# Four small moves in the order of transfers and splits of a fused attention and MLP kernel

## The chip, the cores and the metric

The kernel runs on one core of a Trainium2 chip. The metric is the time of one execution in microseconds of device time, the median of several. All data are float32; matmuls take operands that are split into a high and a low part (fp32r), so that one product is three matmuls.

## The reference, cut to what matters

```
xn  = layernorm(x)                                  # x: 1 x 2048 x 512
qkv = xn @ wqkv                                     # 32 heads of 16
p   = softmax(q k^T / 4)                            # per head, 2048 x 2048
s   = (p v) @ wo
h   = relu(xn @ w1 + b1) ** 2                       # 2048 x 1792
g   = silu(h @ w2 + b2)
out = x + s * g
```

## The kernel before

**Work.** Attention is cut into 32 units: a unit is four heads (a quad, `qd`) and 512 queries (`qc`), so u = 4 qd + qc. A unit has two passes over the keys. The max pass (`max_mm`, L308) multiplies a Q tile `qm` with a K tile `ka` and lets VectorE take the maximum over 512 keys (L323). When a unit's 64 maxima are there, `shift` (L352) turns them into a negated shift, which is stored to DRAM (`keep`, L362, the tensor `sh_d`) and fetched back into rows 48 and 49 of the unit's two exp tiles `qe` (`back`, L367, by `shift_rows`, L377, four transfers of 4 KB). The exp pass (`exp_mm`, L1179) multiplies `ka` with `qe`; the added rows subtract the maximum, and ScalarE takes the exp of it (L1199) into a tile `pt`. `pv_step` multiplies the exps with V two slots later (L387).

**Slots.** The main loop (L1528) counts slots `st`; 16 slots are one unit of the exp pass. A unit's max pass runs some 24 slots ahead (`LEAD`), counted as g = st + 24. In the loop, slots 4 to 451 also hold the MLP, in blocks of four slots (`long_slots`) and single slots; slots 454 to 485 hold the first part of the output projection (`wo_part`, L710), two slots to a tile of 128 rows; from slot 486 on there is no max pass left. In the two slots of `PAIR` (484 and 485) the last four max matmuls are done; the string `order` there says in which sequence exp matmuls ("s") and max matmuls ("m") stand beside the projection's own nine.

**The lead.** Before the loop, `lead_rounds` (L1316) runs the rest of the QKV projection in rounds of one matmul in either half of the array, with max matmuls of the first units and some first exps between them. Six rounds are a step; `now` counts steps there and slots in the loop, and `later(n, fn)` (L198) puts a call off by n of them. Every QKV tile ends in `qk_done` (L998): ScalarE copies it out of PSUM (L1004), POOL splits it into a buffer `hl` of three (L95, L96), SP stores it two steps later (`qk_store`, L942). The last but one tile of the lead, the K columns of the last eight heads, goes through `qk_done_last` (L1008) with its own buffers, and is stored at slot 6 (L1539). The first exp of the lead is in step 45.

**Q loads.** `max_end(g)` (L327) stands at the end of each slot. With s the place of g in its group of 16, it asks for the two exp tiles of unit u (six transfers of 32 KB each, `load_q_pair`) at two places s, and for the two max tiles of unit u + 1 at two others. When a unit's maxima are complete it puts the unit on the list `late` with the g at which `shift` is due. For units after the first the exp tiles' places 12 and 14 are the slots 16u - 12 and 16u - 10, and the places 7 and 9 the slots 16u - 17 and 16u - 15. The max pass is seven slots further ahead than g says, since the lead did 62 max matmuls in either half; it starts on a unit's max tiles in the fourth slot after a multiple of 16.

**Queues.** SP issues nearly all transfers, in the order in which they stand in the program; an issue waits until the data it reads are written, its target is free, and now and then for an earlier transfer. What stands behind it waits too. ScalarE issues only two of the last stores.

**The MLP's start and the projection.** `mlp_tasks` (L467) first calls `load_xc(0)` (L497), which asks in four transfers of 256 KB for the first 256 tokens of the layernorm's result, `xc`; the first MLP block, in slot 4, reads it and the w1 tiles that POOL splits (`split_w1`). The projection asks for its input tiles `oc` in `wo_load` (L665): for the second 512 tokens three of 512 KB, at slots 456, 457 and 458, read from slot 462 on. Between them stand the 13 small loads of `wo_small` (slot 457) and `keep` and `back` of a unit.

Of the kernel before, what the change touches and what calls it, by code (L numbers as in the profile page):

```python
# [10 lines left out]
F32R = mybir.dt.float32r  # L11
# [6 lines left out]
P = 128  # L18
# [9 lines left out]
NU = NQ * 4  # L28
# [25 lines left out]
def kernel(  # L54
# [11 lines left out]
    nc = tc.nc  # L66
# [24 lines left out]
    def split(dst, raw, hi_act=False, lo=None):  # L91
        if hi_act:
            nc.scalar.activation(dst[0], raw, AF.Copy)
        else:
            nc.gpsimd.tensor_scalar(dst[0], raw, 1.0, 0.0, op0=ALU.mult, op1=ALU.add)  # L95
        (lo or nc.gpsimd).tensor_tensor(  # L96
            dst[1], raw, dst[0].bitcast(F32), op=ALU.subtract
        )
# [12 lines left out]
    with ExitStack() as ph:  # L111
# [10 lines left out]
        def ring(name):  # L122
            t = rot[name][turn[name] % len(rot[name])]
            turn[name] += 1
            return t
# [17 lines left out]
        qms = {}  # L143
# [3 lines left out]
        def load_head(t, j, src_d, h, parts, cols):  # L147
            for n, i in enumerate(parts):
                nc.sync.dma_start(
                    t[64 * j + DH * n : 64 * j + DH * (n + 1), :].bitcast(F32),  # L150
                    src_d[h // 8][i, (h % 8) * DH : (h % 8 + 1) * DH, cols],
                )

        def load_k(qd, n):

            p, j, i = n // 6, n // 3 % 2, n % 3
            if n % 6 == 0:
                kas[qd, p] = ring("ka")
            h = 4 * qd + 2 * p + j
            nc.sync.dma_start(  # L160
                kas[qd, p][64 * j + DH * i : 64 * j + DH * (i + 1), :].bitcast(F32),
                k_d[h // 8][i % 2, (h % 8) * DH : (h % 8 + 1) * DH, :],
            )
# [20 lines left out]
        def load_q_pair(u, name, p, tiles):  # L184
                qd, qc = divmod(u, 4)
                t = ring(name)
                for j in range(2):
                    load_head(
                        t, j, q_d, 4 * qd + 2 * p + j, (0, 0, 1), slice(qc * 512, (qc + 1) * 512)
                    )  # L190
                tiles.append(t)

        late = []
# [4 lines left out]
        def later(n, fn):  # L198
            if n:
                waiting.append((now[0] + n, fn))  # L200
            else:
                fn()
# [124 lines left out]
        def max_end(g):  # L327
            for u in [u for u, n in left.items() if n == 0]:
                del left[u]
                m4 = m4s[u % 2]  # L330
                nc.vector.tensor_reduce(m4[:, :16], mxs[u], axis=AX.X, op=ALU.max)
                mxs[u] = m4
                late.append((g + (6 if u else 2), u))
            u, s = divmod(g, 16)
            if u >= NU:
                return
            qd, qc = divmod(u, 4)
            if qc == 2 and qd + 1 < NQ and s % 2 == 0:
                load_k(qd + 1, s // 2)
            if qc == 3 and qd + 1 < NQ and s % 2 == 0 and s < 8:  # L340
                load_k(qd + 1, 8 + s // 2)
            at = (12, 14) if u else (7, 8)
            if s in at:
                load_q_pair(u, "qe", at.index(s), qes.setdefault(u, []))
            if s in (6, 10) and u + 1 < NU:
                load_q_pair(u + 1, "qm", s // 10, qms.setdefault(u + 1, []))

        def shift_due(g):
            if late and late[0][0] <= g:
                shift(late.pop(0)[1])  # L350

        def shift(u):  # L352
            tr = sp.tile([P, 32], F32, name="tr", bufs=1)
            nc.vector.transpose(tr, mxs[u])
            sh = sp.tile([P, 2, 32], F32R, name="sh", bufs=1)
            nc.vector.tensor_scalar(sh[:, 0], tr, -1.0, None, op0=ALU.mult)
            nc.vector.scalar_tensor_tensor(
                sh[:, 1], tr, -1.0, sh[:, 0].bitcast(F32),
                op0=ALU.mult, op1=ALU.subtract,
            )  # L360

            def keep():  # L362
                nc.sync.dma_start(
                    sh_d[u].rearrange("b c i n -> (b c) i n"), sh.bitcast(F32)
                )

            def back():  # L367
                for p in range(2):
                    for i in range(2):
                        shift_rows(u, p, i)  # L370

            later(1, keep)
            later(2, back)

        to_block = []

# [90 lines left out]
        def mlp_tasks(mp):  # L467
# [29 lines left out]
            def load_xc(c):  # L497
                    xc = xp.tile([P, 2, KO, CW], F32R, name="xc")
                    for k in (0, 2) if c == 0 else (0,):
                        kos = slice(k, k + 2 if c == 0 else KO)  # L500
                        for i in range(2):
                            nc.sync.dma_start(
                                xc[:, i, kos].bitcast(F32), xn_d[i, :, kos, c * CW : (c + 1) * CW]
                            )
                    state["xc"] = xc
# [402 lines left out]
        pools = {}  # L908
# [30 lines left out]
        def qk_store(m, c, hl):  # L939
            cs = slice(c * 512, (c + 1) * 512)  # L940
            dst = q_d[m] if m < 4 else k_d[m - 4]
            nc.sync.dma_start(dst[:, :, cs].rearrange("i p n -> p i n"), hl.bitcast(F32))  # L942
# [64 lines left out]

        def qk_done_last(m, c, ps):  # L1008

            hl = pools["n"].tile([P, 2, 512], F32R, name="hl")  # L1010
            raw = sp.tile([P, 512], F32, name="ot", bufs=1)
            nc.scalar.activation(raw, ps, AF.Copy)
            split((hl[:, 0], hl[:, 1]), raw)
            last_store.append(lambda: qk_store(m, c, hl))

        def qk_first():
            tiles = [qk_tile(m, 0) for m in (4, 0)]
# [97 lines left out]
        last_store = []  # L1115
# [47 lines left out]
        order = []  # L1163
# [58 lines left out]
        for i in range(NT + 3):  # L1222
# [38 lines left out]
            if i >= 7 and (i - 3) % 4 == 3:  # L1261
                c = (i - 3) // 4
# [3 lines left out]
            if i >= 3 and (i - 3) % 4 == 3:  # L1266
                c = (i - 3) // 4
# [22 lines left out]
        at = order.index(("v", 2, 0)) + 1  # L1290
# [120 lines left out]
        def slot(st, mms, post):  # L1411

            g = st + LEAD
            lane = (st + flip[0]) % 2
            kb0 = st - lane
            for kb in (kb0, kb0 + 1):
                pts.setdefault(kb, {})
            spare = st >= LAST_MAX
            ex = [
                lambda j=j, kb=kb: exp_mm(kb, j, pts[kb], spare and next(odd))  # L1420
                for kb in (kb0, kb0 + 1) for j in (1 - lane, 3 - lane) if j not in pts[kb]
            ]
            if st in TWO:

                for _ in range(2):
                    max_mm(lane)
                    ex.pop(0)()
                if ex:
                    kb, j = (kb0 + 1, 2 + lane) if lane else (kb0, lane)
                    exp_mm(kb, j, pts[kb], True)  # L1430
                    ex.pop(0)()
                last_use[0] = None
                max_end(g)
                return
            k = 0 if spare else max(0, (8 - len(mms)) // 2)
            own = [lambda: max_mm(lane) for _ in range(k)] + mms
            if spare and lane == 0:

                own.append(lambda: exp_mm(kb0, 0, pts[kb0], next(odd)))
            assert k == 0 or st not in PAIR  # L1440
            mx = [] if spare else [lambda: max_mm(1 - lane) for _ in range(2 if st in PAIR else 4 - k)]
            order = "s" * len(ex) if spare else {0: "smsmsmsm", 1: "smsmssm"}[k]
            if not spare and post is None:

                if k == 0:
                    order = "msmsmsms"
                elif lane and k == 1 and to_block:
                    order = "smsmsms"
            if st in PAIR:
                order = "smsmss"  # L1450
            other = [(ex if o == "s" else mx).pop(0) for o in order]
            other[-1:-1] = [None] * (len(own) - len(other))
            use = None
            for i in range(len(other)):
                if i < len(own):
                    own[i]()
                if spare and lane == 0 and i == len(mms) - 1:

                    use = nc.vector.tensor_scalar(seen, done_d[0][:, :1], 1.0, 0.0, op0=ALU.mult, op1=ALU.add)
                if other[i] is not None:  # L1460
                    follow = other[i]()
                    if i >= len(own) - 1 and use is None:
                        use = follow
            last_use[0] = None if post is not None or spare and lane else use
            if post is not None:
                post()
            max_end(g)
# [117 lines left out]
```

## Time and profile before

| what | us |
|---|---|
| median of 3 runs | 1646.31 (1646.17 to 1649.19) |
| the profiled execution, as a run | 1644.67 |
| its span, first to last instruction | 1642.6 |
| TensorE busy in the span | 1619.3 (99%) |
| VectorE busy | 1359.5 (83%) |
| ScalarE busy | 1190.1 (72%) |
| POOL busy | 523.0 (32%) |
| mean granted TensorE clock | 0.997 |

The profile is one execution. A row of its timeline has the start, the duration, the engine, the line, and in brackets the idle time of that engine just before and what ended it. Groups of equal neighbours are one row (x6). SPq and ACTq are DMA requests as these engines issue them: the time there is that of the issue, not of the transfer. PE is TensorE's matmuls and PEld its weight loads. The granted clock is the share of full speed that TensorE was given.

### The profile page before, as it was taken

Reading aid. Unit: us, or ns where it says so; the run is one execution under the profiler, and the core shown is the slowest. Engines: PE = TensorE matmul, PEld = TensorE weight load, DVE = VectorE, ACT = ScalarE, POOL = GpSimd, SP = SyncE. Lnnn points to the kernel's source line nnn. Section 1 sums busy time; section 2 is a strip of 40 time slices with the busy share of each in tenths; the row PEclk is TensorE's granted clock in tenths of the full one; section 3 lists DMA queues with packets and bytes.
Section 4 is the critical chain, followed back from the end, with each engine's and each line's share of the span. In section 5 each row is a group of like instructions: output and inputs, shape, how many; then the busy total and the mean of one; then the engine's idle time right before and its main releaser. Section 6 shows DMA issues by size and latency. Waiting matters only on the chain.

```text
span 1642.6 us, 36131 instructions
## 1 busy us (share of the span) xinstructions
PE 1619.3 (99%) x13684; PEld 940.6 (57%) x13684; DVE 1359.5 (83%) x2346; ACT 1190.1 (72%) x2351; POOL 523.0 (32%) x547
## 2 busy tenths in 40 slices
PE   7999999999999999999999999999999999999998
PEld 6898665556555654664466456645655565454543
DVE  6486788888888888888888888888888889886744
ACT  7212677777777777877777777777777777776786
POOL 6436568122212311331133112311321224125421
PEclk9999999999999999999999999999999999999999
DMA  6787565424332433433343324323532353137554
GB/s 226 217 277 248 186 184 153 132 85 126 77 106 82 128 80 87 127 90 82 100 122 107 87 74 141 102 67 87 147 97 67 85 150 81 54 114 218 168 179 154
DMA packets 163941, 209.22 MB, mean 127 GB/s; under 512 B 59448, under 2 KB 78392, under 8 KB 162232
## 3 DMA queue, kind: packets, MB, share of 16 engines
q1 hardware_dynamic: 163480, 206.40, 43.1%
q8 instruction: 108, 1.77, 0.4%
q14 instruction: 65, 0.53, 0.1%
q10 hardware_dynamic: 288, 0.52, 0.1%
HBM read 149.95 MB, written 56.61 MB: 126 GB/s over the span
## 4 chain that ended last, share of the span: by engine, by line
PE 96%; DMA 2%; DVE 1%; SPq 0%; issue 0%; ACT 0%; DVEq 0%; ACTq 0%
PE po L387 31%; PE pd_t L254 19%; PE pm_t L316 16%; PE se L1187 14%; PE pd_t L222 6%; PE pm_t L1065 3%; PE se L1035 1%; PE pd_t L1065 1%; PE se L987 1%; PE se L316 1%; DVE mx L323 1%; DMA oc<-on_d 1%; PE pm_t L1187 0%; DMA sh_d<-sh 0%; PE pm_t L1149 0%; PE pd_t L1035 0%
## 5 line engine op out<-in xcount | busy, mean ns | idle before, releaser
L323 DVE TENSOR_REDUCE mx<-pm_t 128x1 f32<-128x512 f32 x1927 | 1197.3, 684 | 172.8 <-PE pm_t L316 86.7
L1199 ACT ACTIVATE pt<-se 128x512 f32<-128x512 f32 x1996 | 1043.3, 617 | 261.8 <-PE se L1187 217.2
L316 PE MATMUL pm_t<-ka,qm 64*128 64x512 f32 x1927 | 770.5, 420 | 0.7 <-DVE mx L323 0.5
L1187 PE MATMUL se<-qe,ka 64*128 64x512 f32 x1996 | 672.6, 396 | 0.9 <-DMA qe<-sh_d 0.6
L387 PE MATMUL po<-pt,v 128*32 128x512 f32 x4096 | 546.1, 605 | 0.0
L316 PEld LDWEIGHTS pm_t<-ka,qm 64*128 64x128 f32 x1927 | 338.5, 184 | 239.0 <-DVE mx L323 226.8
L254 PEld LDWEIGHTS pd_t<-xc,w1s 64*128 64x128 f32 x2688 | 334.2, 187 | 96.6 <-issue 89.3
L254 PE MATMUL pd_t<-xc,w1s 64*128 64x256 f32 x2688 | 380.9, 288 | 1.7 <-DMA xc<-xn_d 0.8
L1187 PEld LDWEIGHTS se<-qe,ka 64*128 64x128 f32 x1996 | 337.2, 185 | 19.1 <-ACT pt L1199 1.2
L254 PE MATMUL pd_t<-w2t,hT 64*128 64x512 f32 x1080 | 300.5, 410 | 0.0
L254 PEld LDWEIGHTS pd_t<-w2t,hT 64*128 64x128 f32 x1080 | 179.1, 184 | 82.8 <-issue 75.5
L545 POOL TENSOR_TENSOR r<-r 128x512 f32<-128x512 f32 x56 | 58.2, 1040 | 376.5 <-ACT r L542 376.5
L387 PEld LDWEIGHTS po<-pt,v 128*32 128x32 f32 x4096 | 81.0, 108 | 159.1 <-issue 136.5
L564 POOL TENSOR_TENSOR u<-u,b_t 128x512 f32<-128x512 f32 x16 | 20.6, 1286 | 327.2 <-ACT u L563 293.3
L425 POOL TENSOR_TENSOR ot<-ot,hl 128x512 f32<-128x512 f32 x31 | 39.8, 1284 | 204.4 <-DMA hl<-r_d 160.3
L323 DVE TENSOR_REDUCE mx<-se 128x1 f32<-128x512 f32 x121 | 77.9, 686 | 30.8 <-PE se L316 25.7
L222 PE MATMUL pd_t<-wot,oc 64*128 64x512 f32 x336 | 92.0, 410 | 3.8 <-DMA oc<-on_d 3.5
L222 PEld LDWEIGHTS pd_t<-wot,oc 64*128 64x128 f32 x336 | 58.9, 186 | 51.5 <-ACT pt L1199 12.6
L542 ACT ACTIVATE r<-pd_t,b_t 128x256 f32<-128x256 f32 x112 | 46.9, 470 | 57.1 <-PE pd_t L254 57.1
L1065 PE MATMUL pm_t<-xT,wr_t 64*128 64x512 f32 x408 | 75.0, 391 | 0.0
L96 POOL TENSOR_TENSOR hT<-r,hT 128x512 fp32r<-128x512 f32 x56 | 72.3, 1290 | 4.7
L222 PE MATMUL pd_t<-w2t,hT 64*128 64x512 f32 x264 | 68.8, 393 | 0.0
(131 smaller groups left out, 1066.1 us busy)
## 6 DMA issues: line engine op xcount, KB each, us to landing
w1s<-w_d SPq DMA_DIRECT2D x196, 256.0 KB
qm<-q_d SPq DMA_DIRECT2D x384, 32.0 KB
ka<-k_d SPq DMA_DIRECT2D x96, 128.0 KB
qe<-q_d SPq DMA_DIRECT2D x384, 32.0 KB
k_d<-hl SPq DMA_DIRECT2D x16, 512.0 KB
q_d<-hl SPq DMA_DIRECT2D x16, 512.0 KB
xn_d<-xT SPq DMA_DIRECT2D x8, 1024.0 KB
g<-g_d SPq DMA_DIRECT2D x32, 256.0 KB
```

What stands on the lines that cost most here:

```text
L96: (lo or nc.gpsimd).tensor_tensor(dst[1], raw, dst[0].bitcast(F32), op=ALU.subtract)
L222: mm = nc.tensor.matmul(out_, lh(r), rh(r), start=first_ and lane == 0, stop=last_ and lane == 1, skip_group_check=True,)
L254: mm = nc.tensor.matmul(out_, lh(r), rh(r), start=first_ and lane == 0, stop=last_ and lane == 1, skip_group_check=True,)
L316: nc.tensor.matmul(ps, qms[u][p][64 * j : 64 * j + 64, qb * P : (qb + 1) * P], kas[qd, p][64 * j : 64 * j + 64, kc * 512 : (kc + 1) * 512] ...
L323: return nc.vector.tensor_reduce(mxs[u][:, c, kc : kc + 1], ps, axis=AX.X, op=ALU.max)
L387: nc.tensor.matmul(po[32 * j : 32 * j + 32, :], vs[qd][:, (4 * kb + j) * VW : (4 * kb + j) * VW + 32], pts[j], start=(kb == 0), stop=(kb = ...
L425: nc.gpsimd.tensor_tensor(ot, ot, hl[:, 1].bitcast(F32), op=ALU.mult)
L542: nc.scalar.activation(r[:, i], ps[:, i * CW : (i + 1) * CW], AF.Relu, bias=b1_t[:, fo : fo + 1])
L545: nc.gpsimd.tensor_tensor(r, r, r, op=ALU.mult)
L1065: mm = nc.tensor.matmul(out_, lh(r), rh(r), start=first_ and lane == first, stop=last_ and lane != first, skip_group_check=True,)
L1187: nc.tensor.matmul(se, kas[qd, j // 2][b : b + 64, kb * P : (kb + 1) * P], qes[u][j // 2][b : b + 64, :], start=True, stop=True,)
L1199: return nc.scalar.activation(pts[j], se, AF.Exp, scale=0.25)
```

## The change

Five edits, none of which adds or removes an arithmetic instruction or a transfer:

1. The first unit's `shift` is due at once when its maxima are complete instead of two groups later (its DVE work and `keep` come two steps earlier), and its `back` comes six steps after it instead of two, so two steps later than before.
2. The exp tiles of every unit but the first two are asked for at places 7 and 9 instead of 12 and 14, the max tiles at 8 and 11 instead of 6 and 10. For u = 1 the places stay; for u = 0 they are 7 and 9 (before: 7 and 8) and 8 and 11 (before: 6 and 10).
3. The four transfers of the first `xc` are issued by ScalarE.
4. `qk_done_last` still copies its tile out at the end of the lead, but POOL splits it at slot 6, and it is stored at slot 9.
5. In the slots of `PAIR` the order ends with a max matmul instead of an exp matmul, and the exps stand further apart.

```diff
@@ max_end
-                late.append((g + (6 if u else 2), u))
+                late.append((g + (6 if u else 0), u))
...
-            at = (12, 14) if u else (7, 8)
+            at = (12, 14) if u == 1 else (7, 9)
             if s in at:
                 load_q_pair(u, "qe", at.index(s), qes.setdefault(u, []))
-            if s in (6, 10) and u + 1 < NU:
-                load_q_pair(u + 1, "qm", s // 10, qms.setdefault(u + 1, []))
+            at = (6, 10) if u == 1 else (8, 11)
+            if s in at and u + 1 < NU:
+                load_q_pair(u + 1, "qm", at.index(s), qms.setdefault(u + 1, []))
@@ shift
             later(1, keep)
-            later(2, back)
+            later(2 if u else 6, back)
@@ load_xc
-                            nc.sync.dma_start(
+                            (nc.sync if c else nc.scalar).dma_start(
                                 xc[:, i, kos].bitcast(F32), xn_d[i, :, kos, c * CW : (c + 1) * CW]
                             )
@@ qk_done_last
-            hl = pools["n"].tile([P, 2, 512], F32R, name="hl")
             raw = sp.tile([P, 512], F32, name="ot", bufs=1)
             nc.scalar.activation(raw, ps, AF.Copy)
-            split((hl[:, 0], hl[:, 1]), raw)
-            last_store.append(lambda: qk_store(m, c, hl))
+
+            def store():
+                hl = pools["n"].tile([P, 2, 512], F32R, name="hl")
+                split((hl[:, 0], hl[:, 1]), raw)
+                later(3, lambda: qk_store(m, c, hl))
+
+            last_store.append(store)
@@ slot
             if st in PAIR:
-                order = "smsmss"
-            other = [(ex if o == "s" else mx).pop(0) for o in order]
+                order = "sms_s_s_m"
+            other = [None if o == "_" else (ex if o == "s" else mx).pop(0) for o in order]
```

## The prediction

> **What bounds the kernel now.** I read the stretches of the profile first, then TensorE's waits, then the timeline of every engine around each gap.
>
> ```profile
> span 1642.6 us, 36131 instructions
> ```
>
> ```profile
> 0.00:16.00 16.00, 7.78 (x37) 6.71 (x38) 10.39 (x41) 10.65 (x20) 9.75 (x14) 1.00 0.88 305
> 135.00:139.00 4.00, 3.43 (x32) 2.64 (x28) 3.11 (x5) 0.60 (x1) 0.90 (x1) 1.00 0.04 7
> 141.00:150.00 9.00, 6.57 (x45) 6.07 (x43) 3.16 (x5) 2.17 (x4) 7.86 (x11) 0.81 0.90 307
> 176.00:182.00 6.00, 4.90 (x34) 1.81 (x32) 4.24 (x9) 2.74 (x6) 5.49 (x9) 1.00 1.03 344
> 400.00:800.00 400.00, 400.00 (x3482) 219.70 (x3476) 356.14 (x609) 309.40 (x616) 93.15 (x92) 1.00 0.36 98
> 1491.00:1496.00 5.00, 1.46 (x15) 0.62 (x15) 1.67 (x4) 1.26 (x3) 2.26 (x3) 1.00 0.63 186
> 1496.00:1501.00 5.00, 5.00 (x30) 2.49 (x33) 2.21 (x5) 2.71 (x5) 4.67 (x5) 0.66 0.98 331
> 1625.00:1642.60 17.60, 12.13 (x99) 6.54 (x95) 8.68 (x15) 4.80 (x11) 2.55 (x2) 0.91 0.35 123
> ```
>
> Columns: stretch, length, busy us of PE, PEld, DVE, ACT and POOL, granted clock, DMA share, GB/s. TensorE sets the time: in 400 to 800 it has no gap at all. What it loses lies at the start (8.2 us), at the end (5.5 us), and in three places between, around 142, 180 and 1493. The change touches only these three and the order of SP's queue. After two of them the granted clock drops as well (0.81, 0.66), so a gap costs more than its idle time. I therefore measure each place by the beat of a repeated matmul.
>
> **Part 1: the first unit's shift asked for 2 steps sooner, fetched 2 steps later** (steps of the lead, 6 rounds each).
>
> ```profile
> 129.99 3.94 SPq L363 DMA_DIRECT2D sh_d<-sh  x1
> 136.37 2.24 SPq L378 DMA_DIRECT2D qe<-sh_d  x4
> 138.72 0.38 SPq L942 DMA_DIRECT2D k_d<-hl  x1
> ```
>
> ```profile
> 141.72 0.62 POOL L95 TENSOR_SCALAR hl<-raw 128x512 fp32r<-128x512 f32 x1 [5.82 <-DMA k_d<-hl]
> ```
>
> ```profile
> 143.73 0.60 ACT L1004 ACTIVATE raw<-pm_t 128x512 f32<-128x512 f32 x1 [7.20 <-POOL hl L96]
> 144.22 0.59 ACT L1199 ACTIVATE pt<-se 128x512 f32<-128x512 f32 x1
> ```
>
> ```profile
> 133.18 0.39 PE L316 MATMUL se<-ka,qm 64*128 64x512 f32 x1
> ...
> 136.39 0.39 PE L316 MATMUL se<-ka,qm 64*128 64x512 f32 x1
> ...
> 138.00 0.39 PE L316 MATMUL se<-ka,qm 64*128 64x512 f32 x1
> ...
> 138.97 0.47 PE L1187 MATMUL se<-qe,ka 64*128 64x512 f32 x1 [0.57 <-DMA qe<-sh_d]
> ...
> 144.87 0.79 PE L316 MATMUL se<-ka,qm 64*128 64x512 f32 x1 [2.43 <-ACT pt L1199]
> ...
> 147.94 0.48 PE L316 MATMUL se<-ka,qm 64*128 64x512 f32 x2
> ```
>
> Read it backwards. TensorE waits 2.43 us for the first exps; ScalarE's first exp stands behind a copy that waits 7.20 us for POOL; POOL waits 5.82 us for a buffer whose store (k_d, 138.72) stands on SP behind the fetch of the shift. SP held that fetch until 136.37 because the shift's own store, issued at 129.99 behind three weight loads and V, had not landed. Meanwhile the DMA engines were at a share of 0.04 (135 to 139): the queue was blocked, not full. Two steps take 136.39 - 133.18 = 3.21 us; from 136.39 to 147.94 are four steps (pairs at 138.00, about 140.5, 144.87, 147.94), 11.55 us instead of 6.42. **The loss is 5.1 us**: 0.57 + 2.43 idle, the rest in slow matmuls.
>
> The Trainium skill ("TensorE: Matmul & The Clock Gate", the part on the clock gate) has the clock halve after an idle window of about 3.4 us, so by it a 2.43 us gap may cost only itself and the loss would be 3.0, the sum below 2.1 smaller. The row disagrees (0.81 after 2.43 us), and the row decides.
>
> With the change the store goes out ahead of the three loads and V, and has from step 33 to step 38, 5 x 1.6 = 8 us, to land before the fetch is due. The k_d store then stands ahead of the fetch and follows V at about 130; even if its issue is held as the shift's store was (3.94 us) it is out at 134, 4.7 us sooner than 138.72. POOL resumes near 137, ScalarE's copy ends near 140, and the exps no longer meet TensorE's limit at 142.4. The fetch (four issues, 2.24 us) is out by 134.9 to 136.5; the last exp operand must be there at 138.4 (138.97 less 0.57). That is tight, so I leave 0.5 of the 5.1: **gain 4.6**, bounds 0 and 5.1. The lead's Q loads one group later (places 7, 9 and 8, 11 instead of 7, 8 and 6, 10) issue the same 24 requests, long ahead of use; the late ones also leave one store ahead of them. Nothing, either way.
>
> **Part 2: xc asked for by ScalarE; part 3: the last K tile's split 4 slots later.**
>
> ```profile
> 175.48 0.42 SPq L942 DMA_DIRECT2D k_d<-hl  x1
> 175.99 3.33 SPq L502 DMA_DIRECT2D xc<-xn_d  x4
> ```
>
> ```profile
> 178.33 1.06 PE L387 MATMUL po<-pt,v 128*32 128x512 f32 x8
> ...
> 183.16 0.38 PE L254 MATMUL pd_t<-xc,w1s 64*128 64x256 f32 x1 [0.56 <-DMA xc<-xn_d]
> ...
> 184.91 1.06 PE L387 MATMUL po<-pt,v 128*32 128x512 f32 x8
> ...
> 187.03 1.06 PE L387 MATMUL po<-pt,v 128*32 128x512 f32 x8
> ...
> 190.61 1.07 PE L387 MATMUL po<-pt,v 128*32 128x512 f32 x8
> ```
>
> ```profile
> 176.21 1.20 ACT L1199 ACTIVATE pt<-se 128x512 f32<-128x512 f32 x2
> ```
>
> ```profile
> L889 ACTq DMA_DIRECT2D out_dram<-g x2: 338/359/380, 1636.4 to 1638.9; - x2
> ```
>
> The same half block takes 190.61 - 187.03 = 3.58 us when nothing waits; the first took 184.91 - 178.33 = 6.58: **3.0 us lost**, waiting for xc. It could be 3.0 at most. But from 176 to 182 the DMA engines were full (share 1.03, 344 GB/s), with two 512 KB stores and xc's 1 MB, so another queue does not make the bytes come much sooner. ScalarE is no earlier either: its first exp in the loop starts at 176.21 and SP asked at 175.99. Its four issues cost between 4 x 0.36 (L889) and 3.33 us (SP's four) on ScalarE, ahead of four exps; with three score banks in flight that delays the last score matmul of slot 3 by about 1 us, which today's wait for xc covers; uncovered it would be a loss of up to 1.5. Gain between -1.5 and 3.0; I take **0.5**, near the row of the full engines.
>
> The Trainium skill ("DMA: Bandwidth & Descriptors", Issuing engines are not separate DMA queues) speaks against this edit: it saves only the sequencer's time. By it alone the term is 0 and the sum 0.5 smaller.
>
> The moved split is two POOL instructions, 1.9 us, and a store moved from slot 6 to 9; POOL's w1 splits come 1.9 us sooner, but xc is what ends that wait. Its K columns are for the last two quads. Nothing.
>
> **Part 4: the Q loads of units 2 and on at places 7, 9 (exp) and 8, 11 (max).**
>
> ```profile
> 1466.47 2.75 SPq L149 DMA_DIRECT2D qe<-q_d  x6
> ...
> 1471.29 3.00 SPq L149 DMA_DIRECT2D qe<-q_d  x6
> ```
>
> ```profile
> 1475.77 1.00 PE po L387 x8
> ...
> 1479.06 1.00 PE po L387 x8
> ...
> 1482.35 0.99 PE po L387 x8
> ...
> 1486.79 8.21 DMA oc<-on_d
> ...
> 1500.89 0.99 PE po L387 x8
> ```
>
> ```profile
> 1495.05 0.50 PE L222 MATMUL pd_t<-wot,oc 64*128 64x512 f32 x1 [3.54 <-DMA oc<-on_d]
> ```
>
> A projection slot beats at 3.29 us (1475.77, 1479.06, 1482.35). The next four took 1500.89 - 1482.35 = 18.54 instead of 13.16: **5.4 us lost**, of which 3.54 idle, waiting for the third oc tile, asked for at 1486.79. SP was then 10 us behind TensorE and, from 1471.29 on, issued without a break. The change takes both sets of six Q loads out of this stretch (slots 452 and 454) to slots 447 and 449, where TensorE has no gap. The second set alone is 3.00 us; the first, 2.75, lay partly in time in which SP would have waited anyway. So oc is asked for 3.0 to 5.75 us sooner. At an unchanged 8.21 us of landing, 3.0 leaves 0.5 of the stall, too short to lower the clock if the 0.57 us gap at 138.97 is a guide. **Gain 4.9**, bounds 2 (landing stretched) and 5.4.
>
> Elsewhere this part moves 12 requests a unit, none added. Its price is in the rivals.
>
> **Part 5: the PAIR slots 484 and 485 end on a max.**
>
> ```profile
> 1574.60 0.47 PE L222 MATMUL pd_t<-wot,oc 64*128 64x512 f32 x1 [0.26 <-issue]
> ```
>
> The only gap nearby is 0.26 us. A max (0.69) instead of an exp (0.60) ends the wait of the next slot, under 1.06 us of P·V matmuls. Gain **0.2**, bounds -0.3 and 0.5.
>
> **Sum:** 4.6 + 0.5 + 4.9 + 0.2 = 10.2 us. The profiled execution took 1644.67 us, 2.1 outside its span, and stands 1.6 below the median of 1646.31. Less 10.2 it is 1634.5, and on the median's scale **1636.1**.
>
> **Rivals.** *The shift stays in the way:* the fetch lands after 138.4, or the k_d store is held longer; TensorE waits for qe instead of exps. For it: the 3.94 us issue. Against: the idle DMA engines. It loses the 4.6: 1640.7. *The projection still waits:* oc lands late whatever SP does, because a transfer ahead of it is slow (100 to 200 GB/s around the stall). Half of 4.9 is lost: 1638.6. *ScalarE's issues hold the first slots* and xc comes no sooner: 2 us worse than my term, 1638.1. *Max Q tiles come late (the slower side):* a unit's first max tile was asked for at slot 14 and is read from slot 4 of the next group of 16. Now SP waits for slot 15's exps, then issues six loads (2.75) and six more (2.75), 5.5 us, of the four slots of 2.85 us (two in 190.61 - 184.91 = 5.70) until the tile is read: 5.9 us are left for landing. It decides from a landing over 5.9 us, or a queue behind by some us; landings here run from 2.6 (136.37 to 138.97) to 8.21. At 1 us of gap in each of 28 units: 1636 + 28 = 1664; break-even is 0.36 us a unit.
>
> **Chances:** forecast 0.62, the shift 0.12, the projection 0.08, ScalarE 0.08, late max tiles 0.10. All but the last end at 1641 or below. The range is from every bound at its best, 5.1 + 3.0 + 5.4 + 0.5 = 14.0 (1632), to the shift and the ScalarE rival together (1643). About 0.2% (3.3 us) is what this kernel's measurements tell from none: faster 0.83, the same 0.07 (two rivals together, or mild late tiles), slower 0.10.
>
> **What would show it.** Right: no gap of TensorE and a clock near 1.00 in 135 to 150; the k_d store ahead of the fetch on SP; oc's wait gone in the first slots of the projection. Xc's wait remains. Wrong: TensorE waiting for qe, for a store's buffer, or for qm at slot 4 of many units, seen as busy time under 400 in 400 us.

## The result and the profile after

| | before | after |
|---|---|---|
| median of 5 runs (range), us | 1646.31 (1645.98 to 1649.82) | 1639.71 (1637.90 to 1640.65) |
| ratio, 95% interval | | 0.9951 (0.9936 to 0.9965) |
| the profiled execution, as a run, us | 1644.67 | 1639.71 |
| its span, us | 1642.6 | 1637.9 |

The change makes the kernel faster: by the ratio 8.1 us (5.8 to 10.5), by the medians 6.6, by the two profiled executions 5.0. The forecast was 1636.1, the range 1632 to 1643. Parts are numbered below as in the prediction (1 the shift, 2 xc, 3 the last K tile, 4 the Q loads, 5 the PAIR slots), not as in the list of edits.

The first view of after is that of the stretches, with the columns of the prediction:

```profile
135.00:139.00 4.00, 4.00 (x36) 3.59 (x34) 2.61 (x5) 0.60 (x1) 1.06 (x3) 1.00 0.68 240
141.00:150.00 9.00, 8.10 (x65) 6.78 (x67) 4.53 (x7) 2.86 (x7) 8.39 (x11) 1.00 0.85 313
176.00:182.00 6.00, 4.06 (x29) 2.51 (x30) 2.09 (x4) 2.42 (x6) 2.10 (x3) 0.88 0.96 278
320.00:340.00 20.00, 18.25 (x144) 9.62 (x146) 16.69 (x32) 13.21 (x26) 0.00 (x0) 1.00 0.35 93
400.00:1480.00 1080.00, 1080.00 (x9397) 593.74 (x9395) 958.87 (x1634) 836.49 (x1662) 263.15 (x260) 1.00 0.37 99
1485.00:1500.00 15.00, 15.00 (x119) 8.40 (x119) 11.77 (x20) 11.15 (x22) 11.32 (x12) 1.00 0.72 228
```

The gaps near 142 and 1493 have shrunk or gone, the place near 180 is worse (busy 4.06 of 6 where it was 4.90, clock 0.88), and there is a new gap after 320. From 400 to 1480 there is none.

**Start-up first.** Two executions differ before the change can act. ScalarE's copies of the lead show it, first in before, then in after:

```profile
83.56 0.60 ACT L1004 ACTIVATE raw<-pm_t 128x512 f32<-128x512 f32 x1 [2.59 <-PE pm_t L1065]
...
172.50 0.60 ACT L1004 ACTIVATE raw<-pm_t 128x512 f32<-128x512 f32 x1 [2.15 <-PE pm_t L1065]
```

```profile
82.72 0.60 ACT L1005 ACTIVATE raw<-pm_t 128x512 f32<-128x512 f32 x1 [2.60 <-PE pm_t L1070]
...
168.80 0.60 ACT L1005 ACTIVATE raw<-pm_t 128x512 f32<-128x512 f32 x1 [2.15 <-PE pm_t L1070]
```

The first copy is 0.84 us sooner, the last 3.70. Only the difference, **2.9 us, is part 1's gain**; 4.6 was forecast. (In the other kernels below the first copy lies between 82.70 and 84.71; each comparison of two traces here takes that off.)

**Around 142.** SyncE, POOL, ScalarE and TensorE of after, a fence for each:

```profile
128.50 0.59 SPq L172 DMA_DIRECT2D v<-v_d  x1
129.19 5.26 SPq L943 DMA_DIRECT2D k_d<-hl  x1
134.54 2.32 SPq L379 DMA_DIRECT2D qe<-sh_d  x4
```

```profile
138.05 0.62 POOL L95 TENSOR_SCALAR hl<-raw 128x512 fp32r<-128x512 f32 x1 [2.86 <-DMA k_d<-hl]
```

```profile
140.07 0.60 ACT L1005 ACTIVATE raw<-pm_t 128x512 f32<-128x512 f32 x1 [4.25 <-POOL hl L96]
```

```profile
141.21 0.50 PE L316 MATMUL se<-ka,qm 64*128 64x512 f32 x1 [0.39 <-ACT pt L1204]
...
145.54 0.50 PE L1192 MATMUL se<-qe,ka 64*128 64x512 f32 x1 [0.69 <-ACT pt L1204]
```

The fetch no longer stands ahead of the K store, but V does, and the store's issue was held 5.26 us behind it. The same chain as before runs from it, shorter: POOL waits 2.86 us for the buffer (5.82 before), ScalarE's copy 4.25 (7.20), TensorE 0.39 and 0.69 (2.43).

**Around 180.** Before's first matmul of the loop, then ScalarE and TensorE of after:

```profile
175.65 0.49 PE L316 MATMUL pm_t<-ka,qm 64*128 64x512 f32 x1 [0.54 <-DVE mx L323]
```

```profile
171.58 0.40 ACTq L503 DMA_DIRECT2D xc<-xn_d  x1
...
172.01 3.08 ACTq L503 DMA_DIRECT2D xc<-xn_d  x3
175.13 2.07 ACT L1204 ACTIVATE pt<-se 128x512 f32<-128x512 f32 x4 [2.57 <-PE pm_t L316]
```

```profile
172.04 0.49 PE L316 MATMUL pm_t<-ka,qm 64*128 64x512 f32 x1 [0.64 <-DVE mx L323]
...
175.78 0.50 PE L1192 MATMUL se<-qe,ka 64*128 64x512 f32 x1 [0.99 <-ACT pt L1204]
...
178.37 0.38 PE L254 MATMUL pd_t<-xc,w1s 64*128 64x256 f32 x1 [0.67 <-DMA xc<-xn_d]
...
180.61 0.58 PE L254 MATMUL pd_t<-xc,w1s 64*128 64x256 f32 x1 [1.27 <-DMA xc<-xn_d]
...
183.68 1.20 PE L388 MATMUL po<-pt,v 128*32 128x512 f32 x8
```

From the loop's first matmul to the third group of P.V matmuls before took 184.91 - 175.65 = 9.26 us, after 11.64: **2.4 us lost**. ScalarE's queue is in its issues until 175.1, so the four exps come late and TensorE waits 0.99 for them; then it waits for xc twice; then its matmuls take 0.58 instead of 0.38, at half clock.

**Around 321, new.** SyncE and TensorE of after:

```profile
297.42 1.73 SPq L435 DMA_DIRECT2D on_d<-hl  x4
307.12 2.63 SPq L149 DMA_DIRECT2D qe<-q_d  x6
309.79 1.46 SPq L172 DMA_DIRECT2D v<-v_d  x1
311.30 2.14 SPq L503 DMA_DIRECT2D xc<-xn_d  x2
...
314.14 3.96 SPq L149 DMA_DIRECT2D qm<-q_d  x6
```

```profile
321.75 0.46 PE L316 MATMUL pm_t<-ka,qm 64*128 64x512 f32 x1 [1.79 <-DMA qm<-q_d]
```

SyncE issued nothing from 299 to 307: the exp tile's load, now at place 7, waited there for its buffer, and V, xc and the max tile stood behind it. In before TensorE was busy for all of these 20 us (320 to 340), here for 18.25. **1.8 us lost.**

**The projection.** P.V of after:

```profile
1483.29 1.06 PE L388 MATMUL po<-pt,v 128*32 128x512 f32 x8
...
1496.45 1.06 PE L388 MATMUL po<-pt,v 128*32 128x512 f32 x8
```

Four slots in 13.16 us, where before took 18.54: **5.4 us gained**, the whole loss. In the PAIR slots the wait of 0.26 us has gone, so about 0.3 more.

The sum for the two profiles: start-up 0.8, part 1 2.9, the loop's start -2.4, the max tile -1.8, the projection 5.4, PAIR 0.3: 5.2, against the 5.0 measured.

### The profile page after: what moved, and what is told of

Its sections match the earlier page's. It is cut to its first block, busy times and chain, and to the rows that moved or that the text cites. A ratio compares the mean times of both kernels' runs of the same rounds, so it can differ in the third digit from the quotient of the medians.

```text
span 1637.9 us, 36064 instructions
## 1 busy us (share of the span) xinstructions
PE 1617.7 (99%) x13684; PEld 941.6 (57%) x13684; DVE 1358.0 (83%) x2346; ACT 1189.5 (73%) x2351; POOL 523.3 (32%) x547
## 4 chain that ended last, share of the span: by engine, by line
PE 93%; ACT 3%; DMA 2%; SPq 1%; DVE 1%; POOL 1%; issue 0%; ACTq 0%; POOLq 0%; DVEq 0%
PE po L388 30%; PE pd_t L254 19%; PE pm_t L316 17%; PE se L1192 14%; PE pd_t L222 5%; PE pm_t L1070 3%; ACT pt L1204 2%; PE se L1040 1%; PE se L988 1%; DMA xc<-xn_d 1%; PE pd_t L1070 1%; DMA k_d<-hl 1%; PE se L316 1%; SPq L149 0%; PE pm_t L1154 0%; PE pd_t L1040 0%
```

## The experiments

All are timed against the kernel before. The three sets ran on three chips; the medians of before beside them were 1647.13 (28 runs), 1645.93 (11) and 1645.37 (11). Across sets the ratios are therefore the fairer measure.

| kernel | set | runs | median, us | ratio to before, 95% |
|---|---|---|---|---|
| e1: after, part 2 undone | first | 5 | 1637.66 | 0.9944 (0.9926 to 0.9962) |
| e2: before, part 4 alone | first | 10 | 1642.79 | 0.9971 (0.9958 to 0.9984) |
| e4: before, part 1 alone | first | 11 | 1641.57 | 0.9965 (0.9955 to 0.9975) |
| e5: before, part 2 alone | first | 12 | 1648.14 | 1.0001 (0.9985 to 1.0016) |
| e3: after, max tiles at 6 and 10 | second | 6 | 1637.04 | 0.9942 (0.9928 to 0.9957) |
| e6: e1 and e3 together | second | 6 | 1636.72 | 0.9943 (0.9929 to 0.9956) |
| e7: e6, V later | second | 5 | 1636.07 | 0.9936 (0.9923 to 0.9950) |
| e9: after, V later | second | 4 | 1637.37 | 0.9944 (0.9927 to 0.9961) |
| e10: e7, xc by ScalarE | third | 6 | 1635.79 | 0.9942 (0.9928 to 0.9957) |
| e11: e7, parts 3 and 5 undone | third | 5 | 1635.29 | 0.9939 (0.9925 to 0.9953) |

### e4: part 1 alone

Against before:

```diff
-                late.append((g + (6 if u else 2), u))
+                late.append((g + (6 if u else 0), u))
...
-            later(2, back)
+            later(2 if u else 6, back)
```

> The kernel before with part 1 alone (the first unit's shift asked for two steps sooner, fetched two steps later). The prediction's term: 4.6 us faster, 1641.7. Theory from the two traces: of the 5.1 us lost around 142 only about 2.6 come back, since the store of the K tile that POOL waits for is now held behind three weight loads and V instead of behind the fetch: about 1643.7. Whatever the changed kernel gained before that place (its matmuls of step 42 were 1.0 us earlier) isn't there if it came from another part.

5.8 us faster by the ratio (4.1 to 7.4). The stretch of e4:

```profile
132.00:152.00 20.00, 20.00 (x177) 19.93 (x175) 13.33 (x21) 6.24 (x12) 15.76 (x19) 1.00 0.80 273
```

No gap at all (before was busy 17.00 of these 20 us). The first copy is 0.43 us sooner than in before and the last 5.48: the gain is 5.1, all of the loss. The K store's issue was held 3.74 us here and out by 131.26; in after it was out at 134.45. So the forecast of 4.6 holds in this execution, and my reading of the two traces, 2.6, took one execution for the rule. e2 and e5, without part 1, gain 0.7 between the same two copies, so before's own profile had lost 0.7 us more there than theirs.

### e1: part 2 undone, and e5: part 2 alone

e1 against after (e5 is the reverse, against before):

```diff
-                            (nc.sync if c else nc.scalar).dma_start(
+                            nc.sync.dma_start(
```

> The changed kernel with the first xc asked for by SyncE again (part 2 undone, the rest kept). Theory: part 2 is what lost time. In the changed kernel the stretch from the start of slot 2 (172.04) to the P.V matmuls of slot 2 (183.68) took 11.64 us, before 9.26 (175.65 to 184.91), so part 2 costs 2.4 us; without it the stretch goes back to about 9.3 us and the time from 1639.7 to about 1637.3. Rival: the stretch is bound by xc's bytes on full DMA engines whoever asks, and its length changed because slot 2 starts 3.6 us sooner; then it stays near 11.6 and the time near 1639.7.

> The kernel before with part 2 alone (the first xc asked for by ScalarE). Theory (ScalarE's issues hold the exps of slot 2, and SyncE's next loads share the engines with xc): 2.4 us slower than before, about 1648.7, with a wait of TensorE for ScalarE's exps near the second P.V of the loop. The prediction's term: 0.5 us faster, 1645.8. Rival (bound by bytes whoever asks): no change, 1646.3.

e1's median fits the theory, but the interval of its ratio overlaps that of after; e5 is not different from before, where 2.4 us slower was expected; its interval reaches about 2.5 us to either side, so the times decide neither way. The traces say more. TensorE of e1, then SyncE, then POOL:

```profile
172.00 0.50 PE L316 MATMUL pm_t<-ka,qm 64*128 64x512 f32 x1 [0.49 <-DVE mx L323]
...
176.96 0.35 PE L254 MATMUL pd_t<-xc,w1s 64*128 64x256 f32 x1 [0.79 <-POOL hl L95]
...
180.12 0.58 PE L254 MATMUL pd_t<-xc,w1s 64*128 64x256 f32 x1 [0.48 <-DMA xc<-xn_d]
...
183.19 1.17 PE L388 MATMUL po<-pt,v 128*32 128x512 f32 x8
```

```profile
172.34 3.31 SPq L503 DMA_DIRECT2D xc<-xn_d  x4
```

```profile
176.35 0.62 POOL L95 TENSOR_SCALAR hl<-ot 128x512 fp32r<-128x512 f32 x1
```

With SyncE asking again the stretch takes 183.19 - 172.00 = 11.19 us, not 9.3: the theory is wrong in its size. ScalarE's wait has gone, and the matmuls still end at half clock. TensorE of e5:

```profile
174.87 0.50 PE L316 MATMUL pm_t<-ka,qm 64*128 64x512 f32 x1 [0.83 <-DVE mx L323]
...
178.54 0.50 PE L1187 MATMUL se<-qe,ka 64*128 64x512 f32 x1 [0.92 <-ACT pt L1199]
...
185.31 1.06 PE L387 MATMUL po<-pt,v 128*32 128x512 f32 x8
```

Here ScalarE's issues cost the same wait (0.92), the clock stays, and the stretch takes 10.44. The stretch in all kernels sorts itself by two things:

| xc asked for by | clock holds | clock drops |
|---|---|---|
| SyncE | before 9.26, e2 9.92 | e1 11.19, e4 11.33, e6 10.90, e7 10.80, e11 11.29 |
| ScalarE | e3 9.64, e5 10.44, e9 10.42, e10 10.20 | after 11.64 |

Within a column ScalarE costs about 0.6 us (means 10.2 and 9.6; 11.6 and 11.1), and a dropped clock about 1.5. Of after's 2.4 us most is the clock. The 0.6 rests on few traces: e3 is no clean entry, since its first matmul of the loop waits 1.48 us for VectorE (0.49 to 0.83 in the others), ahead of the stretch; without it ScalarE's mean is 10.35 and its cost about 0.8. The drop doesn't come from part 2: e4, in which nothing near 180 was edited, has it too, and so have five of the seven traces with SyncE and one of the five with ScalarE.

The 0.79 us wait in e1 also shows a trap in reading. The profile puts it down to POOL's `hl`, which that matmul doesn't read. From the first xc issue of SyncE to the first matmul on xc it is 4.6 to 4.7 us in every such kernel (172.34 to 176.96; before 175.99 to 180.57; e4 170.45 to 175.07), whatever POOL does. So xc's landing ends this wait.

### e2: part 4 alone, and e3: the max tiles back at places 6 and 10

e2 against before:

```diff
-            at = (12, 14) if u else (7, 8)
+            at = (12, 14) if u == 1 else (7, 9) if u else (7, 8)
...
-            if s in (6, 10) and u + 1 < NU:
-                load_q_pair(u + 1, "qm", s // 10, qms.setdefault(u + 1, []))
+            at = (6, 10) if u < 2 else (8, 11)
+            if s in at and u + 1 < NU:
+                load_q_pair(u + 1, "qm", at.index(s), qms.setdefault(u + 1, []))
```

e3 against after:

```diff
-            at = (6, 10) if u == 1 else (8, 11)
+            at = (6, 10) if u else (8, 11)
```

> The kernel before with part 4 alone (the Q loads of units 2 and on at places 7, 9 and 8, 11; those of the first two units as before). The prediction's term: 4.9 us faster, 1641.4. Theory from the two traces: the projection's slots get back 5.3 us, and one late max tile near 320 us (a wait of 1.8 us) takes 1.8 of it: 3.5 us faster, 1642.8. Rival (the late tile belongs to the sooner start of the loop, not to part 4): 5.3 us faster, 1641.0, with no wait for qm.

> The changed kernel with the max Q tiles of units 2 and on back at places 6 and 10 (the exp tiles stay at 7 and 9). Theory: the late max tile at 321.75 (1.8 us) comes from SyncE waiting at the exp tiles' place 7 with V, xc and the max tile queued behind it; with the max tile asked for at place 6 it stands ahead of that wait. The wait for qm near 321 goes, the projection keeps its even slots, and the time is 1.2 to 1.8 us below the changed kernel's 1639.7. Rival: the wait is due to V's and xc's bytes, which still pass at the same time: then it stays, or turns into a wait for xc or V.

e2 is 4.8 us faster (2.6 to 6.9), an interval that holds the term (4.9), the theory (3.5) and the rival (5.3). The trace tells them apart. P.V comes every 3.29 us through the projection, and the late tile is there too, so it belongs to part 4:

```profile
321.42 0.46 PE L316 MATMUL pm_t<-ka,qm 64*128 64x512 f32 x1 [1.25 <-DMA qm<-q_d]
```

The other two kernels with the new places, e1 and e9, stop at the same matmul for 0.63 and 0.58 us. This is TensorE of e1:

```profile
320.01 0.47 PE L316 MATMUL pm_t<-ka,qm 64*128 64x512 f32 x1 [0.63 <-DVE m L331]
```

The profile puts it down to VectorE's `m`, which this matmul doesn't read. In all four kernels it starts 3.6 to 3.7 us after SyncE's last issue of the tile (in e1 that ends at 316.45), so the late tile is the likelier cause, at 0.6 to 1.8 us from one execution to the next.

In e3 the tile's load stands ahead of the one that waits (SyncE of e3):

```profile
292.88 3.59 SPq L149 DMA_DIRECT2D qm<-q_d  x6
...
306.57 2.63 SPq L149 DMA_DIRECT2D qe<-q_d  x6
```

TensorE is busy 20.00 of 20 us from 320 on, and the projection stays whole. The median is 2.7 us below after's and the ratio gives 1.5, with 1.2 to 1.8 expected. The intervals overlap, so the times don't settle it; the trace shows that the wait is gone. So the exp tiles' move alone brings the gain; that of the max tiles brought the late tile.

### e9, e6, e7: V two groups later, and the pieces together

e9 against after; e6 is after with e1's and e3's edits, and e7 is e6 with this one:

```diff
+            if g == 18:
+                load_v(0)
...
                 for fo in range(3):
                     load_w1(fo)
-                load_v(0)
```

> The changed kernel with nothing else than V of the first heads asked for two groups later in the lead. Theory: the K store's issue is held under 3 us instead of 5.26, TensorE waits for no exp between 135 and 150, and the two steps after 137 take 3.21 us each; the time is up to 2 us below 1639.7. Rival: the three weight loads alone hold the store as long; the waits of 0.39 and 0.69 us stay.

> The changed kernel with the first xc asked for by SyncE and the max Q tiles of units 2 and on at places 6 and 10. Theory: it sums e1 and e3, about 1.5 us for the tile and 0.5 to 1.2 us for the issues on ScalarE (from the stretch of slots 2 to 4: 10.44 us with ScalarE against 9.26 and 9.92 with SyncE where the clock stayed at 1.00, 11.64 against 11.19 and 11.33 where it dropped): about 1637. On the clock: each execution seems to have a grid of 3.41 us windows; a window in which TensorE was busy less than about 0.49 is followed by one at half clock, others aren't. The drop near 180 is then there in some executions only.

> As the one before, and V of the first heads asked for two groups later in the lead, so that it stands behind the K store and the fetch of the shift, no longer ahead. Theory: what part 1 left of its loss near 142 (2.2 us in the changed kernel's profile, 0.9 in e1, none in e4) is the time that the K store's issue was held behind three weight loads and V (5.26, 2.92 and 3.74 us); without V ahead it is held under 3 us and nothing is lost there in any execution: 0 to 2 us faster than e6, about 1636, with fewer slow executions. Rival: the weight loads hold it as long; no change.

SyncE of e9, then its stretch:

```profile
128.30 0.45 SPq L943 DMA_DIRECT2D k_d<-hl  x1
128.85 2.89 SPq L379 DMA_DIRECT2D qe<-sh_d  x4
...
132.25 0.60 SPq L172 DMA_DIRECT2D v<-v_d  x1
```

```profile
132.00:152.00 20.00, 20.00 (x178) 19.93 (x176) 13.04 (x20) 6.04 (x11) 16.38 (x20) 1.00 0.88 289
```

The store is issued at once. Between the first and the last copy e7, e9, e10 and e11 gain 4.8 to 5.1 us against before; with V ahead it was 2.9 (after), 3.9 (e3), 4.2 (e1), 4.8 (e6) and 5.1 (e4). So it is V that holds the store, not the weight loads, and by different amounts from one execution to the next. In this stretch what stands right behind V is held in all twelve traces: the shift's store (2.96 to 3.94 us in before, e2 and e5), the K store (2.85 to 5.26 in five), or, with V later, the next weight load (2.77 to 3.27 in four). Why V does so, the traces don't tell. Nor does the length of the hold alone set the gain: e6, held 3.78, gained 4.8, e1 and e3, held 2.92 and 2.85, only 4.2 and 3.9.

e6 came out as expected (1636.72 for 1637); e7 is only 0.65 below it, but its five runs lie within 1.2 us, 1635.13 to 1636.31, where after's lie within 2.8 (those of e10 and e11, which also have V later, lie within 3.0 and 2.3, so a smaller spread is not shown). What I expected of the clock fell in part; it is taken up in the last section.

### e10 and e11: the small terms with the large losses gone

e10 is e7 with xc asked for by ScalarE. e11 is e7 with the split of the last K tile back at the end of the lead and its store at slot 6, and the old order in PAIR.

e11 against e7:

```diff
+            hl = pools["n"].tile([P, 2, 512], F32R, name="hl")
...
-            def store():
-                hl = pools["n"].tile([P, 2, 512], F32R, name="hl")
-                split((hl[:, 0], hl[:, 1]), raw)
-                later(3, lambda: qk_store(m, c, hl))
-            last_store.append(store)
+            split((hl[:, 0], hl[:, 1]), raw)
+            last_store.append(lambda: qk_store(m, c, hl))
...
-                order = "sms_s_s_m"
+                order = "smsmss"
```

> As e7_v_later, but the first xc is asked for by ScalarE, as in the change (so it is the change with the max tiles at 6 and 10 and V later). It tells the price of part 2 with the other two losses gone. In all kernels with SyncE the first matmul that reads xc starts 4.6 us after SyncE's first xc issue (171.80 to 176.40 in e6, 171.56 to 176.25 in e7), so that wait is xc's landing, though the profile puts it down to POOL; ScalarE can ask at most 0.8 us sooner (171.58 against 172.34). Theory: slots 2 to 4 take 9.6 to 10.5 us where the clock holds, a wait of about 1 us for exps is there, and the time is within 1 us of e7's 1636.1. Rival (the prediction's term): 0.5 us faster than e7.

> As e7_v_later, with part 3 (the split four slots later) and part 5 (the order of the PAIR slots) undone. The prediction's terms: nothing for part 3, 0.2 us for part 5: 1636.3. Theory: the wait of 0.8 us ahead of the first xc matmul stays as it is with either place of the split, since xc's landing ends it: the same time as e7 within 0.3 us. Rival: POOL's w1 splits, now behind the K tile's split, end that wait: 1 to 2 us slower, the first xc matmul over 5 us after SyncE's first xc issue.

e10 is at 1635.79 and e11 at 1635.29, e7 at 1636.07: no difference that these runs can show. In e11 the first matmul on xc starts at 175.04, 4.67 us after SyncE's first issue, so part 3 is worth nothing; the 0.26 us wait in PAIR is back. In e10 TensorE's wait for exps is there (0.97), but the clock holds.

These three, with the late tile and V's hold gone, are the best versions: 3.6 to 4.4 us below after by their medians, 1.5 to 2.5 by their ratios. The ratios' intervals overlap that of after, so the size is not settled; the runs of e7 and e11 (1634.21 to 1636.52) all lie below the fastest of after, 1637.90, though the sets ran on different chips.

## Why the prediction was right, and where not

**The sum.** 10.2 us was forecast and 8.1 (5.8 to 10.5) measured. The singles e4, e2 and e5 give 5.8, 4.8 and -0.2, the terms 4.6, 4.9 and 0.5. The two profiled executions bear out less: their places add up to 4.4 (2.9 - 2.4 - 1.8 + 5.4 + 0.3). Before's profiled execution, 1644.67, is faster than all five of its timed runs (1645.98 and up); what those runs lost on top, no trace shows. So the chains of parts 1 and 4 were right, but that the total came so near is in part luck.

**Part 1** was right in its chain and its size was off in the profiled execution, 2.9 for 4.6. The step: "even if its issue is held as the shift's store was (3.94 us) it is out at 134, 4.7 us sooner". It was held 5.26 us there and was out at 134.45, which is 135.3 with the start-up's 0.84 put back: 1.3 us later than forecast, and POOL resumed 1.9 later (138.9 for 137). I took one measured hold for a constant; it ran from 2.85 to 5.26 while V stood ahead, and in e4 (3.74) the whole loss came back. The fetch was in time: no wait for `qe` is left in after. The new places of the first unit's Q loads were not tried alone.

**Part 2** had the wrong sign by the traces; the times leave it open. The step that failed: the delay of ScalarE's exps "which today's wait for xc covers". It wasn't covered: 0.9 to 1.0 us of waiting in after, e5, e9 and e10, before any wait for xc. What came back is the sooner request, at most 172.34 - 171.58 = 0.8 us. The net by the table is a loss of 0.6 to 0.8, inside the bounds. The rule of the Trainium skill ("DMA: Bandwidth & Descriptors", Issuing engines are not separate DMA queues) that another engine saves only the sequencer's time fits better than my term: e10 and e7 don't differ. The rest of the 2.4 us lost there is the clock, which I had priced at the two gaps to be removed and not at the one that stays.

**Part 3** was nothing, as forecast, and for the reason given: xc ends that wait, 4.67 us after SyncE's first issue in e11 too, with POOL's split back at its old place.

**Part 4** gave 5.4 of a possible 5.4 in the projection (4.9 forecast). Of its price the rival of late max tiles had the mechanism, SyncE waiting at the exp tiles with the max tile behind it, and the wrong place: in the other units the time left for landing (5.9 us by the prediction's estimate) was enough, but in one unit V (0.5 MB) and xc (1 MB) stood in the same queue between them. That could be seen in the program's order, and I didn't walk it through for the units in which V is loaded.

**Part 5** brought 0.26 in the profile, forecast 0.2. It was not the only gap there: a second wait, of 0.28 us for exps, follows it in before (1575.84), and it stayed in after (1571.17). The times can't show a term this small.

## What to carry to other kernels

When a load that must wait for its buffer is moved ahead in an in-order queue, list everything that will stand behind it in every unit, the rare large loads first. Keep large transfers out of the queue ahead of a store or a load with a deadline, even if the DMA engines are idle: here a load of 544 KB held the store behind it by up to 5.3 us. And after a gap is removed, look at the gap that remains: its price in clock may change though nothing there was edited.

## What the runs showed of the hardware

The granted clock falls on a grid. Stretches of before, cut at the edges of its drops:

```profile
140.99:144.41 3.42, 1.44 (x13) 0.94 (x9) 1.19 (x2) 0.68 (x2) 2.52 (x4) 1.00 1.02 318
144.41:147.82 3.41, 2.96 (x14) 2.96 (x16) 0.69 (x1) 0.40 (x1) 3.24 (x5) 0.50 0.71 255
```

```profile
1496.09:1499.50 3.41, 3.41 (x16) 1.49 (x12) 0.70 (x2) 1.21 (x3) 3.16 (x4) 0.50 0.99 315
```

e2, with nearly the same gap, and e6:

```profile
139.46:142.88 3.42, 1.69 (x15) 1.25 (x11) 1.29 (x2) 0.66 (x2) 2.49 (x4) 1.00 1.00 308
142.88:146.29 3.41, 2.93 (x25) 2.93 (x27) 1.45 (x3) 0.43 (x1) 3.24 (x5) 1.00 0.69 255
```

```profile
176.44:179.85 3.41, 1.95 (x13) 1.27 (x15) 0.69 (x1) 1.08 (x2) 1.28 (x1) 1.00 0.69 216
179.85:183.26 3.41, 3.41 (x27) 2.48 (x23) 2.07 (x3) 1.79 (x3) 0.00 (x0) 0.50 0.20 43
```

A drop lasts 3.41 us at exactly half clock, and the two of before start 1496.09 - 144.41 = 1351.68 us apart, 396 times 3.413. The grid's place differs from one execution to the next. Taken over the twelve traces, leaving out start and end, a window of the grid in which TensorE was busy 0.44 or less was followed by a drop each time (7 of 7), one of 0.60 or more never; of those from 0.49 to 0.58 four of seven were. (Near the end, three windows of 0.46, 0.48 and 0.59 were followed by none.) My bound of 0.49 was too low (e6: 1.95 of 3.41 us, 0.57, and a drop). So, as an estimate from these rows, a gap of 1.5 to 2.5 us may or may not cost up to half of 3.41 us more, by where it falls on the grid; e2 (busy 1.69 of 3.42 us) got through its 2.21 us gap without a drop, before (1.44) didn't through its 2.43. The Trainium skill ("TensorE: Matmul & The Clock Gate", Part 1) has free-running windows of 3413 ns, which these rows bear out. It lets the clock fall after an idle window; here windows with TensorE busy up to 0.58 of the time were enough.
